# The second score product of an LSH attention read as bf16 halves of f32 words

## The chip, the cores and the metric

One core of a Trainium2 chip runs the whole program in one launch. The metric is the device time of one execution in microseconds; the median of three runs of the kernel before is 961.33 us (959.22 to 962.11).

## The reference

For four batches and eight heads, q, k and v are 768 x 64 in f32. Each row of q and k is hashed into six bits, the signs of its products with a 64 x 6 matrix; a query sees only keys with the same six bits.

```python
q_bits = (einsum(q, proj) > 0);  k_bits = (einsum(k, proj) > 0)      # six bits each
mask   = q_bucket[:, :, :, None] == k_bucket[:, :, None, :]
scores = where(mask, (q @ k.T) / sqrt(64), -1e9)
attn   = exp(scores - max(scores)); attn = attn / (sum(attn) + 1e-9)
x      = (attn @ v)                      # heads side by side: 3072 x 512
h      = maximum(x @ w_in, 0)            # 512 -> 2048
out    = (s * h * h + b) @ w_out         # 2048 -> 512
```

## The kernel before

The work is cut into 32 visits (batch and head) and each visit into three chunks of 256 queries: 96 slots of two tiles of 128 queries. Every result of a matmul goes through one PSUM tile, `bank`, with eight banks of 512 f32 columns.

*Scores* (`weights`, L600 to L650). For a tile of 128 queries the 768 keys are taken in two halves `g` of 384 columns, each in a bank of its own. A half is one accumulation of two matmuls with f32r operands, and this pair is one step of the plan. q and k are both split into a high part, rounded to f32r, and the rest, the low part. L615 multiplies 128 rows: the high part of q, twice (`aq`, the weights), with the high part of k and under it the low part of k (`ks[0]`). L616 multiplies 76 rows: the low part of q in rows 0 to 63 and twelve rows of masks (`bq[0:HR]`, the weights), with the high part of k and twelve mask rows (`ks[1][0:HR]`). The mask rows hold 0 and plus or minus 2^30, so a pair of different hashes gets a large negative score. `bq` and `ks` are f32r tiles that DVE, ACT and DMAs fill in `prep`; they lie in SBUF as four-byte words. There are 192 tiles, 384 halves, and so 384 matmuls each of L615 and L616, each with a weight load of its own.

VectorE then takes the maximum of both halves (L620), ScalarE the exponential and its sum (L621), GpSimd divides (L640). In the first ten visits the attention weights are transposed on TensorE (L672) and multiplied with v in f32 (L680); in the others they are split into two f16 parts (L647, L648), transposed by DMA (L649) and multiplied with v in f16 (L686, L692).

*The MoE layers* (`moe`). The first layer is three f16 matmuls per product, of 256 columns (L788 to L790); the second is f32r with 512 columns (L815). Both have 128 x 128 weights. This work is offered to the planner between the slots and fills TensorE behind the scores; after the last score at 786 us only it is left.

*The order.* All steps are first collected in a `Plan` with an engine, a cost in microseconds, the buffers that they read and write, and a priority. `order` (L73) then plays the program through with these costs and writes down the order in which each engine gets its steps; the engines' instruction streams follow this list. The cost of a score step is given at L617 by `mmc(HS, 2)`, that is 2 x (384 / 2286 + 0.0075) = 0.351 us. The sequence of L615 and L616 inside a step is fixed, and the two steps `g` of a tile have the same priority.

Of the kernel before, what the change touches and what calls it, by code (L numbers as in the profile page):

```python
# [14 lines left out]
BF16 = mybir.dt.bfloat16  # L15
# [153 lines left out]
def lsh_attention_moe(ctx: ExitStack, tc, q, k, v, proj, w_in, w_out, s, b, out):  # L169
    nc = tc.nc  # L170
# [5 lines left out]
    HS = S // 2  # L176
# [7 lines left out]
    HR = D + MR  # L184
# [10 lines left out]

    def f32(ap):
        return ap.bitcast(F32)

    def tile_(name, shape, dt=F32):
        return const.tile(shape, dt, name=name)  # L200

    def dma(dst, src, r, w, pr, size=0):

        plan.add(SP, 0.7, lambda: nc.sync.dma_start(f32(dst()), f32(src())), r, w, pr, size / RATE_DMA)

    def pe(cost, fn, r, w, pr):
        plan.add(PE, cost, fn, r, w, pr)

    def dve(n, fn, r, w, pr, ns=None):
        plan.add(DVE, ((n + 64) / 960.0 if ns is None else ns), fn, r, w, pr)  # L210

    def act(n, fn, r, w, pr, more=0.0, late_=0.0):
        plan.add(ACT, 0.21 + n / 1470.0 + more, fn, r, w, pr, late_)

    def pool(n, fn, r, w, pr, ns=None):
        plan.add(POOL, (0.08 + n / 430.0 if ns is None else ns), fn, r, w, pr)
# [14 lines left out]
    def mmc(n, c):  # L231
        return c * (n / 2286.0 + 0.0075)
# [26 lines left out]
    def late(w):  # L259
        return w >= FULL  # L260

    def TK(r, part, n):

        k = 6 // n
        return [("t", r, z) for z in range(part * k, (part + 1) * k)]

    def tring(i):

        return (i - PAIR) % 3 if i >= PAIR else i % 2
# [8 lines left out]
    def ering(j):  # L278

        return j % NE if late(slots[j // TPC][3]) else j % (NE + 2)  # L280
# [34 lines left out]
    pjk, pjq, pjm = [pjs[:, z] for z in range(3)]  # L315
    nc.vector.tensor_copy(pjh, pj[:, 0])
    nc.vector.tensor_tensor(pjl, pj[:, 0], f32(pjh), ALU.subtract)
    nc.vector.tensor_copy(pjk[0:D], pj[0:D, 1])
    nc.vector.tensor_copy(pjk[D:P], pj[D:P, 0])
    nc.vector.tensor_tensor(pjm[0:D], pj[0:D, 1], f32(pjk[0:D]), ALU.subtract)  # L320
    nc.vector.tensor_copy(pjq, pj[:, 1])
    nc.vector.tensor_tensor(pjq[D:P], pj[D:P, 1], f32(pjq[D:P]), ALU.subtract)
# [127 lines left out]
    def AK(x, r=(0, 1), g=(0, 1)):  # L450
        return [("aq", x, i, j) for i in r for j in g]

    def BK(x, r=(0, 1), g=(0, 1)):
        return [("bq", x, i, j) for i in r for j in g]

    def KK(x):
        return [("ks", x, i, g) for i in range(3) for g in range(2)]
# [142 lines left out]
    def weights(i, pr):  # L600

        bb, h, c, w = slots[i]
        x, y = w % 2, i % NST
        aq, bq, ks = AQ[x], BQ[x], KS[x]
        nm, z, rz, u, big_ = [st[:, y, m] for m in range(5)]
        nk, zk = [[("st", y, m, a) for a in range(TPC)] for m in range(2)]
        for a in range(TPC):
            t, j = c * TPC + a, TPC * i + a
            b0 = (6 if i < EARLY else TWO if late(w) else 0) if j % 2 else 0
            bk = [("b", b0), ("b", b0 + 1)]  # L610
            ts = slice(t * P, (t + 1) * P)
            for g in range(2):
                def mm(g=g, ts=ts, b0=b0):
                    cols, o = slice(g * HS, (g + 1) * HS), bank[:, b0 + g, 0:HS]
                    nc.tensor.matmul(o, aq[:, ts], ks[0][:, cols], start=True, stop=False)  # L615
                    nc.tensor.matmul(o, bq[0:HR, ts], ks[1][0:HR, cols], start=False, stop=True)  # L616
                pe(mmc(HS, 2), mm, AK(x) + KK(x) + BK(x), [bk[g]], pr)  # L617
            e, ek = EB[ering(j)], EK[ering(j)]
            sc = bank[:, b0:b0 + 2, 0:HS]
            dve(S, lambda a=a, sc=sc: nc.vector.tensor_reduce(nm[:, a:a + 1], sc, AX.XY, ALU.max, negate=True), bk, [nk[a]], pr, 0.88)  # L620
            act(S, lambda a=a, sc=sc, e=e: nc.scalar.activation(e.rearrange("p (g n) -> p g n", g=2), sc, AF.Exp, bias=nm[:, a:a + 1], accum_out=z[:, a:a + 1]),  # L621
                bk + [nk[a]], [ek, zk[a]], pr, 0.15, 0.2)

        def missing():
            nc.gpsimd.tensor_scalar(big_, nm, -FLOOR, 1e30, ALU.is_gt, ALU.mult)  # L625
            nc.gpsimd.tensor_scalar(u, nm, -FLOOR, 1.0 / (S + EPS), ALU.is_gt, ALU.mult)
        pool(TPC, missing, nk, [("st", y, 3), ("st", y, 4)], pr, 0.7)

        def inverse():
            nc.vector.scalar_tensor_tensor(rz, z, EPS, big_, ALU.add, ALU.add)  # L630
            nc.vector.reciprocal(rz, rz)  # L631
        dve(1, inverse, zk + [("st", y, 4)], [("st", y, 2)], pr, 0.32)
        for a in range(TPC):
            j = TPC * i + a
            e, ek = EB[ering(j)], EK[ering(j)]
            n, r = j % 2, tring(i)
            hi, lo, hk = pb[:, n, 0], pb[:, n, 1], EK[NE + n]

            def norm(eng, a=a, e=e):
                eng.tensor_scalar(e, e, rz[:, a:a + 1], u[:, a:a + 1], ALU.mult, ALU.add)  # L640
            ways = [(POOL, NORM, lambda norm=norm: norm(nc.gpsimd))]
            if not late(w) and not POOLN:
                ways.append((ACT, 0.93, lambda a=a, e=e: nc.scalar.activation(e, e, AF.Identity, bias=u[:, a:a + 1], scale=rz[:, a:a + 1])))
            plan.any(ways, [("st", y, 2), ("st", y, 3)], [ek], pr)
            if not late(w):
                continue
            act(S, lambda e=e, hi=hi: nc.scalar.mul(hi, e, TOP), [ek], [hk], pr)  # L647
            dve(S, lambda e=e, hi=hi, lo=lo: nc.vector.scalar_tensor_tensor(lo, e, TOP, hi, ALU.mult, ALU.subtract), [ek, hk], [("lo", n)], pr, 1.0)  # L648
            plan.add(SP, TCOST, lambda a=a, n=n, r=r: nc.sync.dma_start_transpose(tb[:, r, a].rearrange("p h t q -> p (h t) q"), pb[:, n].rearrange("p h n -> p (h n)")),  # L649
                     [hk, ("lo", n)], TK(r, a, 2), pr, TLAG)  # L650
# [206 lines left out]
    for i in range(NSL):  # L857
        pr = 10.0 * i
        bb, h, c, w = slots[i]
        last = c == NCH - 1  # L860
        if last and w + 2 < len(visits):
            parts = prep(w + 2, i, pr)
        if c == h == 0 and bb + 1 < B:
            value_scale(bb + 1, pr + VLATE)
        weights(i, pr + WP)
        while nd[0] < min(ND, decodes(i)):
            decode(nd[0], pr + 15)
            nd[0] += 1
        now, parts = (parts, []) if not last else (parts[:2], parts[2:])
        values(i, pr + 5, now)  # L870
        for bb, h, c, w in [slots[x] for x in closed]:
            last = c == NCH - 1
            if last and w + 2 < len(visits):
                prep_values(w + 2, pr + 12)
            if h == H - 1:
                todo.append(moe(bb, c, 0, PASS if bb == 0 else NF // 4))
                if bb == 0 and last:
                    todo.extend(moe(bb, c2, PASS, NF // 4) for c2 in range(NCH))
        closed.clear()
        while todo and next(todo[0], True):  # L880
            todo.pop(0)
# [66 lines left out]
```

## Time and profile before

| | |
|---|---|
| median of three runs | 961.33 us |
| profiled execution | 960.13 us |
| its span, first to last instruction | 958.3 us |
| TensorE matmul busy | 921.6 us, 96% |
| ScalarE, GpSimd, VectorE busy | 656.7, 614.2, 606.2 us |
| L615, 384 matmuls | 146.7 us busy, mean 382 ns |
| L616, 384 matmuls | 132.1 us busy, mean 344 ns |

The profiled execution is one run, with 1.8 us outside its span. Matmuls are pipelined: the next starts before the end that is drawn for the one before, so a mean duration is longer than the distance between two starts, and it is the distances that add up to time. A weight load (PEld) is an instruction of its own and can run while the matmul before is still streaming. "Issue" as a releaser means that an engine waited for nothing that the profile shows.

### The profile page before, as it was taken

The numbers are of one execution on the slowest core, as the hardware profiler recorded it, in microseconds if no ns is written. First come the engines' busy times: TensorE is split into PE (matmuls) and PEld (weight loads), VectorE is DVE, ScalarE is ACT, GpSimd is POOL, SyncE is SP. The second block draws the span as 40 slices with busy tenths as digits, with TensorE's granted clock in tenths as the row PEclk, the third lists the DMA queues.
The fourth block names the chain that finished last, engine by engine and source line by source line (L and its number), as shares of the span: only waits on it lengthen the run. The fifth ranks groups of instructions, "written<-read, shape, count | busy, mean of one in ns | idle before, by whom it ended". The sixth has DMA issues, their size and how long they took to land.

```text
span 958.3 us, 18093 instructions
## 1 busy us (share of the span) xinstructions
PE 921.6 (96%) x6512; PEld 733.2 (77%) x6512; DVE 606.2 (63%) x1001; ACT 656.7 (69%) x1234; POOL 614.2 (64%) x706
## 2 busy tenths in 40 slices
PE   7999887999999999999999999999999999999997
PEld 5876666677667777877878778788778887888886
DVE  7688997888777777776767676768777752000000
ACT  3788886778786777677778777767777775444342
POOL 2467775686896756766777676767667775334332
PEclk8999999899999999999999999999999999999999
DMA  5378657647779898997898798888887875100000
GB/s 123 87 232 220 177 160 191 179 133 209 174 153 204 176 206 181 204 213 149 157 204 172 163 204 163 177 174 167 186 173 149 171 134 105 55 19 27 12 23 23
DMA packets 303721, 144.44 MB, mean 151 GB/s; under 512 B 264256, under 2 KB 286784, under 8 KB 303632
## 3 DMA queue, kind: packets, MB, share of 16 engines
q1 hardware_dynamic: 298432, 126.25, 60.5%
q10 hardware_dynamic: 5200, 17.05, 5.7%
q8 instruction: 51, 0.84, 0.3%
q14 instruction: 38, 0.31, 0.1%
HBM read 51.38 MB, written 14.16 MB: 68 GB/s over the span
## 4 chain that ended last, share of the span: by engine, by line
PE 70%; DVE 9%; POOL 7%; ACT 5%; issue 5%; DMA 2%; POOLq 0%; SPq 0%; ACTq 0%; DVEq 0%
PE bank L815 22%; PE bank L788 7%; PE bank L790 7%; PE bank L789 7%; PE bank L615 6%; PE bank L616 5%; PE bank L686 4%; PE bank L680 3%; PE bank L672 2%; PE bank L692 2%; POOL eb L640 2%; DVE st L620 2%; PE bank L485 2%; POOL glb L802 2%; ACT eb L621 1%
## 5 line engine op out<-in xcount | busy, mean ns | idle before, releaser
L640 POOL TENSOR_SCALAR eb<-eb,st 128x768 f32<-128x768 f32 x176 | 200.4, 1145 | 68.4 <-DVE st L631 51.8
L815 PE MATMUL bank<-w,ghb 128*128 128x512 f32 x768 | 213.6, 406 | 0.0
L788 PE MATMUL bank<-xc,wi 128*128 128x256 f16 x768 | 211.6, 276 | 0.3 <-ACT rb L798 0.3
L620 DVE TENSOR_REDUCE st<-bank 128x1 f32<-128x768 f32 x192 | 180.3, 952 | 49.6 <-PE bank L616 42.3
L790 PE MATMUL bank<-xc,wi 128*128 128x256 f16 x768 | 209.7, 273 | 0.0
L789 PE MATMUL bank<-xc,wi 128*128 128x256 f16 x768 | 209.7, 273 | 0.0
L621 ACT ACTIVATE eb<-bank,st 128x768 f32<-128x768 f32 x176 | 157.5, 896 | 65.2 <-DVE st L620 29.3
L801 POOL TENSOR_SCALAR rb<-rb,misc 128x512 f32<-128x512 f32 x96 | 84.8, 884 | 154.0 <-ACT ghb L800 146.4
L648 DVE SCALAR_TENSOR_TENSOR pb<-eb,pb 128x768 f16<-128x768 f32 x132 | 144.3, 1097 | 61.5 <-ACT pb L647 60.9
L798 ACT ACTIVATE rb<-bank,dsc 128x512 f32<-128x512 f32 x95 | 65.2, 687 | 149.1 <-PE bank L790 135.4
L615 PE MATMUL bank<-ks,aq 128*128 128x384 f32 x384 | 146.7, 382 | 10.8 <-ACT eb L621 5.2
L815 PEld LDWEIGHTS bank<-w,ghb 128*128 128x128 f32 x768 | 136.1, 189 | 21.2 <-issue 0.4
L802 POOL TENSOR_TENSOR glb<-rb,ghb 128x512 fp32r<-128x512 f32 x96 | 137.1, 1428 | 5.8
L616 PE MATMUL bank<-ks,bq 76*128 76x384 f32 x384 | 132.1, 344 | 0.8 <-DMA bq<-nat 0.8
L647 ACT ACTIVATE pb<-eb 128x768 f16<-128x768 f32 x132 | 110.1, 836 | 14.3 <-DMA tb<-pb 13.3
L815 PE MATMUL bank<-w,glb 128*128 128x512 f32 x384 | 113.0, 402 | 3.1 <-POOL glb L802 3.1
L788 PEld LDWEIGHTS <-wi 128*128 128x128 f16 x768 | 75.0, 98 | 44.5 <-issue 37.3
L615 PEld LDWEIGHTS bank<-ks,aq 128*128 128x128 f32 x384 | 74.5, 194 | 30.0 <-ACT eb L621 9.2
L838 DVE COPY osb<-bank 128x256 f32<-128x256 f32 x4 | 1.5, 420 | 133.7 <-PE bank L815 133.0
L815 PEld LDWEIGHTS bank<-w,glb 128*128 128x128 f32 x384 | 70.8, 189 | 19.5 <-POOL glb L802 4.9
L625 POOL TENSOR_SCALAR st<-st 128x2 f32<-128x2 f32 x96 | 41.8, 436 | 63.2 <-DVE st L620 58.4
L790 PEld LDWEIGHTS <-wi 128*128 128x128 f16 x768 | 75.2, 98 | 8.6
(137 smaller groups left out, 1510.2 us busy)
## 6 DMA issues: line engine op xcount, KB each, us to landing
ks<-aq SPq DMA_DIRECT2D x60, 192.0 KB
raw<-in_moe_w_in_dram ACTq DMA_DIRECT2D x16, 512.0 KB
raw<-in_moe_w_out_dram ACTq DMA_DIRECT2D x16, 512.0 KB
xc<-xd SPq DMA_DIRECT2D x60, 128.0 KB
nat<-in_q_dram SPq DMA_DIRECT2D x32, 192.0 KB
nat<-in_k_dram SPq DMA_DIRECT2D x32, 192.0 KB
vm<-in_v_dram SPq DMA_DIRECT2D x32, 192.0 KB
xd<-xsb SPq DMA_DIRECT2D x48, 128.0 KB
```

The lines of the kernel that those rows point to most:

```text
L615: nc.tensor.matmul(o, aq[:, ts], ks[0][:, cols], start=True, stop=False)
L616: nc.tensor.matmul(o, bq[0:HR, ts], ks[1][0:HR, cols], start=False, stop=True)
L620: dve(S, lambda a=a, sc=sc: nc.vector.tensor_reduce(nm[:, a:a + 1], sc, AX.XY, ALU.max, negate=True), bk, [nk[a]], pr, 0.88)
L621: act(S, lambda a=a, sc=sc, e=e: nc.scalar.activation(e.rearrange("p (g n) -> p g n", g=2), sc, AF.Exp, bias=nm[:, a:a + 1], accum_out=z[: ...
L640: eng.tensor_scalar(e, e, rz[:, a:a + 1], u[:, a:a + 1], ALU.mult, ALU.add)
L647: act(S, lambda e=e, hi=hi: nc.scalar.mul(hi, e, TOP), [ek], [hk], pr)
L648: dve(S, lambda e=e, hi=hi, lo=lo: nc.vector.scalar_tensor_tensor(lo, e, TOP, hi, ALU.mult, ALU.subtract), [ek, hk], [("lo", n)], pr, 1.0)
L788: nc.tensor.matmul(hp, w[:, 0, fs], xc[:, 0, :], start=(cc == 0), stop=False)
L789: nc.tensor.matmul(hp, w[:, 1, fs], xc[:, 0, :], start=False, stop=False)
L790: nc.tensor.matmul(hp, w[:, 0, fs], xc[:, 1, :], start=False, stop=(cc == NC_ - 1))
L802: pool(2 * CH, lambda r=r, gh=gh, gl=gl: nc.gpsimd.tensor_tensor(gl, r, f32(gh), ALU.subtract), [rk, hk], [lk], MP)
L815: nc.tensor.matmul(o, (gh, gh, gl)[z][:, ts], w[:, z % 2], start=(f == fa and z == 0), stop=(f == fz - 1 and z == 2))
```

## The change

L616 reads its two operands as bf16. `top` takes a four-byte operand, views it as pairs of two-byte values, and selects the second of each pair, which is the upper half of the word: sign, exponent and the first seven bits of the fraction. The values are cut off, not rounded, and nothing is written: the same tiles are read with a step of four bytes. The mask values 0 and plus or minus 2^30 are the same in bf16. L615 stays f32r, and both accumulate into the same f32 bank. The cost of the step in the plan falls by 0.013.

```diff
+    def top(ap):
+
+        return ap.bitcast(BF16).rearrange("p (n t) -> p n t", t=2)[:, :, 1]
+
...
                     nc.tensor.matmul(o, aq[:, ts], ks[0][:, cols], start=True, stop=False)
-                    nc.tensor.matmul(o, bq[0:HR, ts], ks[1][0:HR, cols], start=False, stop=True)
-                pe(mmc(HS, 2), mm, AK(x) + KK(x) + BK(x), [bk[g]], pr)
+                    nc.tensor.matmul(o, top(bq[0:HR, ts]), top(ks[1][0:HR, cols]), start=False, stop=True)
+                pe(mmc(HS, 2) - 0.013, mm, AK(x) + KK(x) + BK(x), [bk[g]], pr)
```

## Rows read from the trace of the kernel before

**Rows 1.** Page, section 1: busy time, share of the span, instructions of each engine.

```profile
PE 921.6 (96%) x6512; PEld 733.2 (77%) x6512; DVE 606.2 (63%) x1001; ACT 656.7 (69%) x1234; POOL 614.2 (64%) x706
```

**Rows 2.** Page, section 2: the span in 40 slices, busy tenths of TensorE.

```profile
PE   7999887999999999999999999999999999999997
```

**Rows 3.** Three windows: length, busy us (instructions), clock, DMA share, GB/s.

```profile
0.00:250.00 250.00, 225.18 (x1749) 175.75 (x1750) 206.99 (x417) 190.11 (x414) 159.82 (x210) 0.96 0.63 171
250.00:786.00 536.00, 529.83 (x3656) 422.47 (x3655) 387.30 (x566) 392.72 (x711) 384.75 (x429) 1.00 0.84 177
786.00:958.30 172.30, 166.58 (x1111) 134.95 (x1110) 11.91 (x20) 73.85 (x112) 69.66 (x69) 1.00 0.17 40
```

**Rows 4.** Chain that ended last, share of the span by line (cut there).

```profile
by line: PE bank L815 21.6%; PE bank L788 7.0%; PE bank L790 6.7%; PE bank L789 6.7%; PE bank L615 6.1%; issue 5.3%; PE bank L616 5.3%; PE bank L686 4.0%; PE bank L680 2.6%; PE bank L672 2.4%; PE bank L692 2.3%; POOL eb L640 2.3%; DVE st L6
```

**Rows 5.** Groups by line: busy us, mean ns; idle before, what ended it.

```profile
L788 PEld LDWEIGHTS <-wi 128*128 128x128 f16 x768 | 75.0, 98 | 44.5 <-issue 37.3 <-DMA xc<-xd 0.3
L616 PEld LDWEIGHTS bank<-ks,bq 76*128 76x128 f32 x384 | 74.8, 195 | 2.8 <-issue 1.1
```

**Rows 6.** Timeline, PE, scores: start us, us, engine, line, operation, tiles, shape.

```profile
503.69 0.34 PE L616 MATMUL bank<-ks,bq 76*128 76x384 f32 x1
...
504.40 0.34 PE L616 MATMUL bank<-ks,bq 76*128 76x384 f32 x1
504.58 0.28 PE L788 MATMUL bank<-xc,wi 128*128 128x256 f16 x1
504.70 0.27 PE L789 MATMUL bank<-xc,wi 128*128 128x256 f16 x1
```

**Rows 7.** Timeline, PE, second layer of the MoE near 850 us, same columns.

```profile
849.22 0.27 PE L790 MATMUL bank<-xc,wi 128*128 128x256 f16 x1
849.25 2.11 PE L815 MATMUL bank<-w,ghb 128*128 128x512 f32 x8
851.20 1.09 PE L815 MATMUL bank<-w,glb 128*128 128x512 f32 x4
852.12 0.28 PE L788 MATMUL bank<-xc,wi 128*128 128x256 f16 x1
852.24 0.27 PE L789 MATMUL bank<-xc,wi 128*128 128x256 f16 x1
...
854.64 0.27 PE L790 MATMUL bank<-xc,wi 128*128 128x256 f16 x1
```

**Rows 8.** Timeline, PE weight loads, end of a group of scores near 512 us.

```profile
511.63 0.19 PEld L615 LDWEIGHTS bank<-ks,aq 128*128 128x128 f32 x1
...
512.16 0.10 PEld L788 LDWEIGHTS <-wi 128*128 128x128 f16 x1 [0.16 <-issue]
512.18 0.10 PEld L789 LDWEIGHTS <-wi 128*128 128x128 f16 x1
```

**Rows 9.** Timeline, PE matmuls of the same stretch.

```profile
511.34 0.27 PE L790 MATMUL bank<-xc,wi 128*128 128x256 f16 x1
...
511.63 0.35 PE L616 MATMUL bank<-ks,bq 76*128 76x384 f32 x1
...
511.99 0.34 PE L616 MATMUL bank<-ks,bq 76*128 76x384 f32 x1
512.17 0.28 PE L788 MATMUL bank<-xc,wi 128*128 128x256 f16 x1
512.29 0.27 PE L789 MATMUL bank<-xc,wi 128*128 128x256 f16 x1
```

**Rows 10.** Timeline, PE, first and last of the 73 places with f16 behind L616.

```profile
152.78 0.34 PE L616 MATMUL bank<-ks,bq 76*128 76x384 f32 x1
...
153.07 0.27 PE L789 MATMUL bank<-xc,wi 128*128 128x256 f16 x1
...
780.41 0.34 PE L616 MATMUL bank<-ks,bq 76*128 76x384 f32 x1
...
780.71 0.27 PE L789 MATMUL bank<-xc,wi 128*128 128x256 f16 x1
```

## The prediction

> **What bounds the kernel now.** I read the busy shares first. TensorE's matmuls are busy for 96% of the span, and no other engine passes 69% [rows 1]. The slices show where the missing 4% lies: in the first quarter and at the very end; from about 300 us to the end nearly every slice is full [rows 2]. [...] "Busy" is padded by pipelining, so I then read the chain of waits: its largest parts are lines of TensorE, and the two score lines, L615 and L616, are 6.1% and 5.3%, together 11.4% of 958.3 us, or 109 us [rows 4]. So a shorter score matmul is worth something in most places, though not in all. The changed line has 384 matmuls, each with a weight load of its own [rows 5]. Drawn durations overlap with their neighbours'; what counts is the distance from one start to the next, and that I read from the timeline.
>
> **The paces.** Five score matmuls in a row, from 503.69 to 504.58, are 0.178 us apart (384 columns, f32r) [rows 6]. Twenty-two f16 matmuls of 256 columns, from 852.24 to 854.64, are 0.1091 us apart. The twelve f32r matmuls of 512 columns before them start when the L790 of 849.22 is through (849.33) and end at 852.12: 2.79 us, 0.2325 each [rows 7]. From 384 to 512 columns f32r thus pays 0.0545 us for 128 columns, and f16 pays 0.1091 / 2 = 0.0546 for 128. The pace per column is the same. What f32r costs more is a fixed piece per instruction: 0.178 less 1.5 times 0.1091 (0.1636) is 0.0144 us.
>
> **The change part by part.**
>
> *The matmul of L616 in bf16.* No row shows a bf16 matmul, or one that reads every other 16-bit word. The lower end of its pace is that of f16 carried to 384 columns, 0.1636 us; the upper end is the present 0.178, as the words lie in memory as before. I take 0.1636: the surplus of f32r does not grow with the columns, so it is not the reading of four bytes per column that costs. Saving: 0.0144 x 384 = 5.5 us of TensorE time.
>
> *The weight load of L616 in bf16.* Its record will shrink from 195 to something near the 98 ns of the f16 loads [rows 5]. That alone is worth nothing, for today it is hidden: the f32r load of L615 at 511.63 starts together with the matmul ahead of it, the L616 of 511.63 [rows 8, 9]. But the f16 load behind an f32r matmul is not hidden. The load of L788 behind the last L616 starts only at 512.16, after 0.16 us without a load, 0.01 us before its own matmul (512.17), whereas the next load, at 512.18, runs beside that matmul [rows 8, 9]. F16 matmuls with 128 columns of weights follow L616 at 73 places, the first at 152.78 and the last at 780.41 [rows 10], and the load row of L788 has 37.3 us of such idle time put down to "issue" [rows 5]. In time: from the last L616 to the second f16 matmul it is 0.30 us at 504.40, 511.99 and 780.41 and 0.29 at 152.78 [rows 6, 9, 10]; the two paces make 0.287. The starts are rounded to 0.01; the mean of the four, 0.2975, puts the uncovered load at 0.0105, and I take 0.011. The other way round, f16 to f32r, costs nothing that shows: from L790 at 511.34 to L616 at 511.63 is 0.29, against 0.287 [rows 9].
>
> Now every L616 stands behind an L615, which stays f32r. After the change 384 two-byte loads will stand behind f32r matmuls, and I expect each to be uncovered as those of L788 are: 0.011 x 384 = 4.2 us that must be paid back. A pair costs 0.0144 - 0.011 = 0.0034 us less than before, 1.3 us in all. The bounds of this term are 0 (the load hidden, as the f32 load is) and 0.098 (the whole record of an f16 load uncovered, 37.6 us in all); I stay with 0.011, the row with the same neighbours.
>
> *What follows L616.* At 73 places f16 work follows, and there the uncovered load of today goes, because two-byte work will stand on both sides: 73 x 0.011 = 0.8 us saved. Where f32r work follows (L615 itself 192 times), the bf16 to f32r step costs nothing, by the row above; its bounds are 0 and the same 0.011.
>
> *The planner.* The cost of a score step falls by 0.013 us, 384 times, 5.0 us of planned TensorE time. The planner picks the order of all five engines from these times, so the order may change anywhere after the first score step. Nothing in the trace prices that; as bounds I take a tenth of the matmul-free 36.7 us (24.8 + 6.2 + 5.7) either way, 3.7 us, and nothing as the value, because it has no preferred sign.
>
> *Nothing else moves.* The operands are read in place: no copy, no DMA, no wait, no new tile; VectorE, ScalarE and GpSimd do what they did. VectorE's maximum waits for the end of L616, which comes 0.003 us sooner.
>
> **The sum.** 1.3 + 0.8 = 2.1 us of TensorE time. The scores take 384 x 2 x 0.178 = 136.7 us, of which 109 are on the chain: a factor of 0.80. That leaves 1.7 us. Against the profiled execution, 960.13 us (958.3 us of span and 1.8 around it), that is 958.4; it ran 1.2 us under the median, so on the median of the runs I say **959.6 us**. What is late next is TensorE again; no other engine is near.
>
> [...]
>
> **The rivals.**
>
> *The load is hidden after all.* If a bf16 load with a step is started ahead as the f32 load at 511.63 is, the full 5.5 us remain, and the 0.8 at the borders with f16: 6.3 x 0.80 = 5.0 us, **956.3**. For it: the cover is there, 0.178 us of L615. Against it: no two-byte load behind an f32r matmul of the scores uses it.
>
> *Slower: the uncovered load takes longer with its step.* The place is the start of each L616, behind L615. If the 0.011 doubles, a pair costs 0.0076 more than now, 2.9 us, less 0.8, times 0.80: +1.7. At three times, 0.033, it is (7.1 - 0.8) x 0.80 = +5.0, **966.3**. It decides from about 0.026 us on, where the loss passes 2.9 us. For it: every two-byte load of the trace reads packed words. Against it: the f32 loads read words at the same places and keep up under matmuls of 0.178 us. The same side is reached if the matmul keeps 0.178: (4.2 - 0.8) x 0.80 = +2.7, 964.0.
>
> *The order decides.* The 0.013 in the planner moves steps so that TensorE waits more or less in the first 250 us: 3.7 off the forecast, 955.9 or 963.3. For it: 24.8 free us there. Against it: 0.013 us is small beside the steps of 0.3 to 1.4 us in the plan.
>
> *The change does not take:* if the operands still went as four-byte words, only the order would differ, **961.3**. The types in the diff speak against that, and I give it next to nothing.
>
> **The chances.** The forecast 0.45, its own range 958 to 961.5; the hidden load 0.20; the longer load, or the unchanged pace, 0.16; the order 0.17, half each way; no effect 0.02. A run of this kernel can tell 0.3%, 2.9 us, from no change; so faster means under 958.4, slower over 964.2. Faster: 0.06 of the forecast, 0.19 of the hidden load, 0.08 of the order: 0.33. Slower: 0.14 of the longer load, 0.05 of the order, 0.01 of the forecast: 0.20. The rest, 0.47, is within. For the range I take in the hidden load with some luck of the order, 954.5, and the longer load at three times, 966.
>
> **What would show it.** In the rows of L616: a matmul of type bf16, with its weight load near 0.1 us. Right, if in the timeline L616's load starts about 0.17 us after L615's matmul and not with it, so that the load row of L616 shows some 384 x 0.15 = 58 us of idle put down to "issue"; if L615 to L616 to the next L615 is 0.354 us; and if the first f16 load behind L616 starts ahead. The first rival shows as a load that starts with L615 and a pair of 0.342; the second as a pair of 0.368 or more. The prediction is wrong if the pair lies at either of these, or if the matmul-free time of the first 250 us differs by more than 3 us.

## The result, and the profile after

The changed kernel takes 972.08 us (median of 6 runs, 969.44 to 973.62), the kernel before 961.72 us beside it: a ratio of 1.0106, 95% interval 1.0089 to 1.0122. The forecast was 959.6 us, no measurable change, with a range from 954.5 to 966. The change makes the kernel 1.1% slower, and it does so by a way that the prediction had priced at nothing.

Lines are shifted by four from here on: L615 and L616 are now L619 and L620, VectorE's maximum L624, ScalarE's exponential L625, the f16 matmuls L792 to L794, the f32r ones of the second layer L819. From the page of the changed kernel, the row of [rows 1] and, at the end, the granted clock in 40 slices:

```profile
span 971.0 us, 18104 instructions
...
PE 930.3 (96%) x6512; PEld 696.5 (72%) x6512; DVE 621.0 (64%) x1017; ACT 654.2 (67%) x1222; POOL 600.1 (62%) x706
...
PEclk7999997799999999999999999999999999999999
```

TensorE is busy for 96% of a span that is 12.7 us longer. In the slices the clock's digit is 7 in the first and in the seventh and eighth, at 146 to 194 us. The windows of [rows 3], for the changed kernel (length, busy us and instructions of PE, PEld, DVE, ACT, POOL, then the clock):

```profile
0.00:250.00 250.00, 219.42 (x1637) 153.68 (x1638) 201.32 (x390) 177.97 (x392) 152.23 (x201) 0.92 0.59 160
250.00:786.00 536.00, 530.75 (x3666) 397.02 (x3665) 398.97 (x596) 393.19 (x704) 367.27 (x428) 1.00 0.88 179
786.00:971.00 185.00, 180.16 (x1213) 145.78 (x1212) 20.73 (x32) 83.04 (x127) 80.63 (x79) 1.00 0.20 46
```

In the first 250 us TensorE is without a matmul for 30.6 us (24.8 before), the granted clock is 0.92 (0.96 before), and 1637 matmuls are done where 1749 were. From 250 to 786 us the two kernels do the same amount, 3666 and 3656. So the kernel falls behind in the first quarter and has 1213 matmuls left after 786 us in place of 1111. The groups that answer to [rows 5], with L620's matmul (busy us, mean ns; idle before):

```profile
L620 PE MATMUL bank<-ks,bq 76*128 76x384 bf16 x384 | 136.0, 354 | 0.0
...
L792 PEld LDWEIGHTS <-wi 128*128 128x128 f16 x768 | 75.3, 98 | 35.5 <-issue 28.0 <-DMA xc<-xd 0.3
...
L620 PEld LDWEIGHTS <-bq 76*128 76x128 bf16 x384 | 38.3, 100 | 54.7 <-issue 38.0
```

The matmul is of type bf16, its load takes 100 ns instead of 195, and there are now 38.0 us of "issue" before it, which were 1.1. The timeline of a group of scores in the changed kernel, matmuls and then their weight loads (start us, duration us):

```profile
540.02 0.34 PE L619 MATMUL bank<-ks,aq 128*128 128x384 f32 x1
540.20 0.35 PE L620 MATMUL bank<-ks,bq 76*128 76x384 bf16 x1
540.24 0.48 PE L619 MATMUL bank<-ks,aq 128*128 128x384 f32 x1
540.56 0.35 PE L620 MATMUL bank<-ks,bq 76*128 76x384 bf16 x1
540.60 0.48 PE L619 MATMUL bank<-ks,aq 128*128 128x384 f32 x1
540.92 0.34 PE L620 MATMUL bank<-ks,bq 76*128 76x384 bf16 x1
```

```profile
540.20 0.10 PEld L620 LDWEIGHTS <-bq 76*128 76x128 bf16 x1 [0.16 <-issue]
540.20 0.20 PEld L619 LDWEIGHTS bank<-ks,aq 128*128 128x128 f32 x1
540.56 0.10 PEld L620 LDWEIGHTS <-bq 76*128 76x128 bf16 x1 [0.15 <-issue]
```

The load of L620 at 540.20 starts with its own matmul, after 0.16 us without a load, and the f32r load behind it starts at once: what [rows 8] showed for L788 now happens before each L620 (all 384 loads start within 0.02 us of their own matmul; in the kernel before none did, and the median load started 0.175 us ahead). From one L620 to the next it is 0.36 us. A pair is one L619 with its L620. From 250 us on, where a pair follows a pair at once, the distance from one second product to the next has a median of 0.363 us (125 places); in the kernel before it is 0.356 (127 places).

### The profile page after: what moved, and what is told of

It reads as the page before. It is cut to its first block, busy times and chain, and to the rows that moved or that the text cites. A ratio compares the mean times of both kernels' runs of the same rounds, so it can differ in the third digit from the quotient of the medians.

```text
span 971.0 us, 18104 instructions
## 1 busy us (share of the span) xinstructions
PE 930.3 (96%) x6512; PEld 696.5 (72%) x6512; DVE 621.0 (64%) x1017; ACT 654.2 (67%) x1222; POOL 600.1 (62%) x706
## 4 chain that ended last, share of the span: by engine, by line
PE 74%; DVE 10%; issue 5%; POOL 5%; ACT 4%; DMA 1%; POOLq 0%; DVEq 0%; SPq 0%; ACTq 0%
PE bank L819 23%; PE bank L792 7%; PE bank L794 7%; PE bank L793 7%; PE bank L619 6%; PE bank L620 6%; PE bank L690 4%; PE bank L684 3%; PE bank L696 2%; DVE st L624 2%; PE bank L676 2%; PE bank L489 2%; POOL glb L806 1%; ACT eb L625 1%; POOL eb L644 1%
## 5 line engine op out<-in xcount | busy, mean ns | idle before, releaser
L644 POOL TENSOR_SCALAR eb<-eb,st 128x768 f32<-128x768 f32 x176 | 191.8, 1096 | 62.1 <-DVE st L635 55.7
L819 PE MATMUL bank<-w,ghb 128*128 128x512 f32 x768 | 221.0, 415 | 0.0
L624 DVE TENSOR_REDUCE st<-bank 128x1 f32<-128x768 f32 x192 | 180.8, 952 | 57.7 <-PE bank L620 50.2
L792 PE MATMUL bank<-xc,wi 128*128 128x256 f16 x768 | 211.2, 275 | 0.8 <-ACT rb L802 0.8
L794 PE MATMUL bank<-xc,wi 128*128 128x256 f16 x768 | 209.8, 273 | 0.0
L625 ACT ACTIVATE eb<-bank,st 128x768 f32<-128x768 f32 x176 | 157.5, 895 | 61.0 <-DVE st L624 35.1
L805 POOL TENSOR_SCALAR rb<-rb,misc 128x512 f32<-128x512 f32 x96 | 81.4, 848 | 149.9 <-ACT ghb L804 142.1
L619 PE MATMUL bank<-ks,aq 128*128 128x384 f32 x384 | 152.2, 449 | 12.4 <-ACT eb L625 6.1
L819 PEld LDWEIGHTS bank<-w,ghb 128*128 128x128 f32 x768 | 136.1, 190 | 21.8 <-issue 1.2
L620 PE MATMUL bank<-ks,bq 76*128 76x384 bf16 x384 | 136.0, 354 | 0.0
L819 PE MATMUL bank<-w,glb 128*128 128x512 f32 x384 | 114.2, 406 | 1.3 <-POOL glb L806 1.3
L792 PEld LDWEIGHTS <-wi 128*128 128x128 f16 x768 | 75.3, 98 | 35.5 <-issue 28.0
L619 PEld LDWEIGHTS bank<-ks,aq 128*128 128x128 f32 x384 | 77.0, 201 | 29.0 <-ACT eb L625 10.0
L629 POOL TENSOR_SCALAR st<-st 128x2 f32<-128x2 f32 x96 | 45.6, 475 | 81.4 <-DVE st L624 70.5
L819 PEld LDWEIGHTS bank<-w,glb 128*128 128x128 f32 x384 | 71.3, 189 | 15.9 <-POOL glb L806 1.8
```

The lines of the kernel that those rows point to most:

```text
L620: nc.tensor.matmul(o, top(bq[0:HR, ts]), top(ks[1][0:HR, cols]), start=False, stop=True)
L792: nc.tensor.matmul(hp, w[:, 0, fs], xc[:, 0, :], start=(cc == 0), stop=False)
L794: nc.tensor.matmul(hp, w[:, 0, fs], xc[:, 1, :], start=False, stop=(cc == NC_ - 1))
L819: nc.tensor.matmul(o, (gh, gh, gl)[z][:, ts], w[:, z % 2], start=(f == fa and z == 0), stop=(f == fz - 1 and z == 2))
```

## The experiments

**Which of the two parts loses.** The diff has two parts, a type and a planned cost. The first kernel keeps the bf16 matmul and takes the cost back, so that each engine has exactly the order of steps of the kernel before:

```diff
-                pe(mmc(HS, 2) - 0.013, mm, AK(x) + KK(x) + BK(x), [bk[g]], pr)
+                pe(mmc(HS, 2), mm, AK(x) + KK(x) + BK(x), [bk[g]], pr)
```

> L616 in bf16 as in the change, but the planned cost of a score step as before (0.351), so that every engine has its steps in the order of the kernel before. Order theory (the loss comes from the order that the cost of 0.338 gives): some 1 to 3 us over the kernel before, 962.5 to 964.5, since a pair of score matmuls is 0.363 us instead of 0.355 in the changed kernel's trace, 0.008 x 384 = 3.1 us, less what the borders with f16 give back. Pace theory (the bf16 matmul makes the loss): 970 or more.

Measured: 961.42 us against 959.67 for the kernel before, ratio 1.0011 (0.9992 to 1.0030). In the trace the sequence of instructions is that of the kernel before on every engine. The second keeps the cost and takes the bf16 back; in the trace its order is that of the changed kernel on every engine:

```diff
-  nc.tensor.matmul(o, top(bq[0:HR, ts]), top(ks[1][0:HR, cols]), start=False, stop=True)
+  nc.tensor.matmul(o, bq[0:HR, ts], ks[1][0:HR, cols], start=False, stop=True)
```

> L616 in f32r as before, but the planned cost of a score step 0.338, so that every engine has its steps in the order of the changed kernel. Order theory: most of the loss is here, 968 to 971. Pace theory: no change from before, 960 to 963.

Measured: 970.02 us, ratio 1.0101 (1.0071 to 1.0131). The order theory holds: the order alone costs 1.0%, of 1.06% in all; the bf16 matmul costs 0.1%, which is not clear of nothing.

**Where the order loses.** Windows of the kernel before, of bf16 in the old order, and of f32r in the new order, in this sequence:

```profile
0.00:100.00 100.00, 90.03 (x691) 71.43 (x692) 80.27 (x166) 72.27 (x165) 55.97 (x87) 0.95 0.61 164
...
150.00:200.00 50.00, 43.77 (x339) 33.43 (x336) 43.04 (x90) 39.10 (x82) 34.84 (x41) 0.93 0.59 153
```

```profile
150.00:200.00 50.00, 43.69 (x342) 31.26 (x341) 42.91 (x89) 38.03 (x80) 33.93 (x40) 0.92 0.61 156
```

```profile
0.00:100.00 100.00, 86.71 (x639) 67.61 (x640) 80.80 (x163) 68.36 (x156) 51.70 (x81) 0.91 0.61 163
...
150.00:200.00 50.00, 39.60 (x263) 28.94 (x261) 34.42 (x68) 30.37 (x65) 25.45 (x31) 0.80 0.55 143
```

In its first 100 us the new order has done 639 matmuls where 691 were done. With the old order the stretch from 150 to 200 us looks as before, bf16 or not: 339 and 342 matmuls at a clock of 0.93 and 0.92. With the new order it has 263 at 0.80, and VectorE, ScalarE and GpSimd are idler too (VectorE 34.4 us busy instead of 43.0): no engine is busier than before, they wait for each other. Two such waits, in TensorE's timeline of the f32r kernel with the new order (in brackets the idle time and what ended it):

```profile
159.56 0.34 PE L620 MATMUL bank<-ks,bq 76*128 76x384 f32 x1
162.18 0.44 PE L619 MATMUL bank<-ks,aq 128*128 128x384 f32 x1 [2.29 <-ACT eb L625]
...
163.84 0.47 PE L676 MATMUL bank<-ident,eb 128*128 128x128 f32 x1 [0.68 <-POOL eb L644]
...
166.76 0.53 PE L620 MATMUL bank<-ks,bq 76*128 76x384 f32 x1
167.08 0.53 PE L619 MATMUL bank<-ks,aq 128*128 128x384 f32 x1
167.40 0.53 PE L620 MATMUL bank<-ks,bq 76*128 76x384 f32 x1
```

```profile
181.18 0.49 PE L489 MATMUL bank<-ident,nat 128*128 128x128 f32 x3
184.71 0.90 PE L489 MATMUL bank<-ident,nat 128*128 128x128 f32 x3 [3.03 <-DVE bq L492]
```

After the L620 of 159.56 the next step in TensorE's list is another score step, whose bank is not free until ScalarE's exponential of an earlier tile is done, and TensorE waits 2.29 us. After the L489 of 181.18 the list has another transposition that waits 3.03 us for VectorE's L492. The same time on VectorE:

```profile
181.53 0.93 DVE L436 SCALAR_TENSOR_TENSOR wi<-raw,wsc,wi 128x512 f16<-128x512 f32 x1
182.49 0.96 DVE L624 TENSOR_REDUCE st<-bank 128x1 f32<-128x768 f32 x1
183.37 0.76 DVE L752 SCALAR_TENSOR_TENSOR xsb<-xpb,vsc,xsb 128x256 f16<-128x256 f32 x1
184.05 0.60 DVE L492 SCALAR_TENSOR_TENSOR bq<-bank,misc,aq 128x384 fp32r<-128x384 f32 x1
```

VectorE's list puts the split of a MoE weight (L436), a maximum (L624) and an output split (L752) ahead of the L492 for which TensorE waits. And the loss has a second part. By the clock's records the granted clock falls to its lower level, 0.50 of full, at 163.3 us, 1.1 us after the end of the long wait and within the next one, and stays there until 177.0 us: from 166.76 to 167.40 the score matmuls are 0.32 us apart, not 0.178. Before 200 us TensorE is at that level for 20.5 us in the kernel before and for 37.5 us here; 6.9 us of the difference lie in the first 28 us. The first row of the page of this kernel, beside [rows 1], divides the loss:

```profile
PE 925.9 (96%) x6512; PEld 735.5 (76%) x6512; DVE 622.6 (64%) x1017; ACT 654.5 (68%) x1222; POOL 603.1 (62%) x706
```

The span is 10.1 us longer (968.4 us). TensorE is without a matmul for 42.4 us in place of 36.7, 5.7 us more, and the same 6512 matmuls are drawn 4.4 us longer. An estimate of the clock's part from the trace alone: matmuls are busy at the lower level for 32.2 us in place of 18.9; if all of them are drawn out there as the score matmuls are, from 0.178 us to 0.32, then 0.44 of the 13.3 us is the clock's, 5.9 us. So waits and clock have about equal parts in these two executions.

**Which stretch of the plan.** Both kernels are f32r; the cut of 0.013 is given to the first 21 slots alone, or to the others alone:

```diff
-  pe(mmc(HS, 2) - 0.013, mm, ...)
+  pe(mmc(HS, 2) - (0.013 if i < EARLY else 0.0), mm, ...)     # the second: 0.0 and 0.013 exchanged
```

> All f32r as before; the planned cost of a score step is 0.338 in the first 21 slots alone (to about 140 us), 0.351 after. Head theory (the loss of the changed order is made in the first 200 us, where TensorE waits and its clock falls): some 5 to 10 us over before, 965 to 970. Spread theory (the loss is summed up over all slots): 960 to 963.

> All f32r as before; the planned cost of a score step is 0.351 in the first 21 slots as before, 0.338 from slot 21 on. Head theory: the order up to some 140 us is that of before, so 959 to 963, unless the stretch from 150 to 200 us is hit by itself. Spread theory: 967 to 970.

Measured: 971.84 us (ratio 1.0116, 1.0089 to 1.0143) with the cut in the first slots, 963.18 us (1.0032, 1.0011 to 1.0052) with the cut in the rest. The head theory holds: a cut in slots up to 140 us is enough for the whole loss. The cut in the rest costs 0.3% by itself.

**Is it the size of the cut?** f32r in all three, with the cost lower by 0.006 and by 0.001, or higher by 0.013:

```diff
-  pe(mmc(HS, 2) - 0.013, mm, ...)
+  pe(mmc(HS, 2) - 0.006, mm, ...)                             # the others: + 0.013, - 0.001
```

> All f32r as before; the planned cost of a score step is cut by 0.006 everywhere instead of 0.013. If the plan answers to the cost smoothly: about half of the loss of order alone, 964 to 966. If any other cost means another order, with a loss that has no relation to the size of the cut: anywhere from 958 to 972, and the half-clock stretches before 200 us go with it.

> All f32r as before; the planned cost of a score step is 0.013 higher, 0.364, about what a pair in the changed kernel takes. If the plan answers smoothly and the cut was wrong because it is too short: faster than before or equal, 950 to 961. If any other cost means another order by chance: 958 to 972.

> All f32r; the planned cost of a score step is cut by 0.001 instead of 0.013. If the plan answers smoothly: 960 to 961.5, no change. If any other cost means another order, and the order of before is one of the better ones: 963 to 973, no nearer to before than the cuts of 0.006 and 0.013.

Measured: 973.72 us (1.0130, 1.0105 to 1.0154), 969.54 us (1.0097, 1.0067 to 1.0128), and, for the cut of 0.001, 976.93 us (1.0164, 1.0145 to 1.0182), the slowest of all. The cuts of 0.006 and 0.001 come out slower than the slowest that was expected of them, 972 and 973. The plan does not answer smoothly, nor to the sign. Each of these costs gave another order, and all six, whole or in part, are slower than that of the kernel before, by 0.3 to 1.6%. The kernel with the cut of 0.001, from 150 to 200 us:

```profile
150.00:200.00 50.00, 41.97 (x299) 31.48 (x299) 33.19 (x70) 31.29 (x68) 26.50 (x34) 0.86 0.54 146
```

299 matmuls at 0.86: the same kind of stretch as with the full cut.

**What the bf16 matmul costs by itself.** Two kernels in the order of before replace one operand of L616 by a packed bf16 tile of zeros, `pk`, and so leave out the second product (two added lines make L620 L622 here):

```diff
-  nc.tensor.matmul(o, top(bq[0:HR, ts]), top(ks[1][0:HR, cols]), start=False, stop=True)
+  nc.tensor.matmul(o, pk[0:HR, 0:P], top(ks[1][0:HR, cols]), start=False, stop=True)      # e3
+  nc.tensor.matmul(o, top(bq[0:HR, ts]), pk[0:HR], start=False, stop=True)                # e4
```

> Order of before, L616 in bf16; its weights are a packed tile of zeros (128 neighbouring two-byte values) instead of every other half of bq, so the low part of q and the masks are left out of the result. If the step of four bytes makes the weight load longer: the pair falls from 0.363 to about 0.354 us, the sum of 0.178, 0.1636 and an uncovered load of 0.011 to 0.013. If the step costs nothing in the load: it stays at 0.363.

> Order of before, L616 in bf16 with its weights read in steps of four bytes as in the change; the moving operand is a packed tile of zeros, so the product of the low part of q and the masks is left out of the result. If the step slows the moving operand: the pair falls from 0.363 to about 0.354 us. If the step costs only in the weight load: it stays at 0.363.

In one execution of each, the medians of 127 distances from one second product to the next, from 250 us on, are 0.365 us with both operands in steps of four bytes (the first experiment), 0.362 with packed weights, 0.357 with a packed moving operand. So it is mostly the moving operand for which the step costs, 0.008 us a matmul; the load has 0.003 of it. The packed tile holds zeros; no run has a packed operand with the real values, so that zeros by themselves are quicker is not ruled out. Two neighbouring second products, first of the kernel with both stepped, then with the moving operand packed:

```profile
529.45 0.35 PE L620 MATMUL bank<-ks,bq 76*128 76x384 bf16 x1
...
529.81 0.34 PE L620 MATMUL bank<-ks,bq 76*128 76x384 bf16 x1
```

```profile
528.40 0.34 PE L622 MATMUL bank<-pk,bq 76*128 76x384 bf16 x1
...
528.75 0.34 PE L622 MATMUL bank<-pk,bq 76*128 76x384 bf16 x1
```

If packed bf16 has the pace of f16, an estimate that no run tests, the 0.357 are 0.178 for f32r, 0.1636 for packed bf16, and 0.015 left for the uncovered load. The same sum with packed weights, 0.362 = 0.178 + 0.172 + 0.012, puts a packed load at 0.012.

**The border itself.** In the order of before, L615 reads the upper halves too; the lower bits of the high parts are then left out of the scores, which become coarser:

```diff
-  nc.tensor.matmul(o, aq[:, ts], ks[0][:, cols], start=True, stop=False)
+  nc.tensor.matmul(o, top(aq[:, ts]), top(ks[0][:, cols]), start=True, stop=False)
```

> Order of before; L615 too reads the upper halves of its four-byte words, so the lower bits of the high parts are left out of the result. If the weight load of L616 is uncovered because f32r stands ahead of it, and the moving operand in steps of four bytes costs 0.008 as the two looks with packed operands say: loads start with the matmul before them again, and a pair takes 2 x 0.172 = 0.344 us. If a two-byte load read in steps of four bytes is always uncovered: 2 x (0.172 + 0.015) = 0.374 us.

Matmuls, then weight loads, of this kernel:

```profile
521.14 0.34 PE L620 MATMUL bank<-ks,bq 76*128 76x384 bf16 x1
...
521.49 0.34 PE L620 MATMUL bank<-ks,bq 76*128 76x384 bf16 x1
...
521.83 0.34 PE L620 MATMUL bank<-ks,bq 76*128 76x384 bf16 x1
...
522.18 0.33 PE L620 MATMUL bank<-ks,bq 76*128 76x384 bf16 x1
```

```profile
521.14 0.10 PEld L619 LDWEIGHTS <-aq 128*128 128x128 bf16 x1
521.32 0.10 PEld L620 LDWEIGHTS <-bq 76*128 76x128 bf16 x1
```

Three pairs in 1.04 us, 0.346 by the median: 0.173 a matmul. The loads start with the matmul before their own, about 0.17 us ahead, as at 521.14. So a two-byte load in steps of four bytes is hidden in this run, where two-byte work stands ahead of it; in the changed kernel, behind f32r, none of the 384 is. The one execution took 951.45 us; more executions, beside the kernel before:

> The kernel of the look with both products in bf16 again, timed: order of before, and the bits of the high parts below the upper half of their words are left out of the scores. Border theory (f32r and two-byte work side by side cost the uncovered load, and bf16 by itself is the cheaper form): a pair of 0.342 to 0.344 us against 0.356 saves 384 x 0.012 = 4.6 us, and more at the borders with f16, so 953 to 957. If the 951.45 of the one look holds, there is a gain beside the pair as well.

Measured: 954.90 us against 960.41, ratio 0.9938 (0.9917 to 0.9959): the gain that the border theory forecast, though the pair is 0.346 us and not 0.342 to 0.344; and the only kernel of the study that beats the one before, at the price of coarser scores.

The last one keeps L615 in f32r and, in the order of before, puts the two L615 of a tile ahead of its two L616 where both halves stand side by side on TensorE:

```diff
-  for each half g, in its own step:  L615(g); L616(g)          # in outline
+  where the two steps are neighbours: L615(0); L615(1); L616(0); L616(1)
```

> Order of before, L616 in bf16; in the 124 tiles whose two halves stand next to each other on TensorE, both L615 come first and then both L616, so that one load in place of two stands uncovered. If an uncovered load costs 0.015 us: 124 x 0.015 x 0.8 = 1.5 us under the ungrouped kernel with the order of before, about 960 and no different from the kernel before. If the border costs nothing by itself: the same as that kernel, 961.4.

Measured: 960.37 us against 961.25, ratio 0.9993 (0.9980 to 1.0006). In its trace 260 loads of the second product start with their own matmul, and the 124 that stand behind another second product start 0.174 us ahead: hidden again, which is the mechanism without a change of type. The time is 0.18% below the ungrouped kernel's 1.0011, as the uncovered load would have it, but the two intervals overlap; it is no different from the kernel before.

## Why the prediction was wrong

*The planner* is the step that failed. The prediction said that "the order may change anywhere after the first score step", bounded that by 3.7 us either way, and took nothing as the value "because it has no preferred sign". Order alone costs 1.0%, some 10 us. Both halves of the argument failed. The bound, a tenth of the matmul-free time (24.8, 6.2 and 5.7 us by the windows of [rows 3]), had no row behind it: matmul-free time alone grew by 5.7 us with the new order, and the bound left out the clock: where 0.50 of it was granted, the score matmuls were 0.32 us apart and not 0.178. And for this kernel the sign was hardly open: six of six other orders lost. The prediction's own sign of being wrong came: the matmul-free time of the first 250 us is 30.6 us against 24.8, 5.8 apart where 3 were allowed. Against the rival "the order decides" it was held that 0.013 us "is small beside the steps of 0.3 to 1.4 us in the plan"; a cut of 0.001 moved the kernel by 1.6%. The rival had its place right, the first 250 us, and its price of 963.3 too low by 8.8 us.

*The weight load* went as foretold: it is uncovered behind L615, as [rows 8] showed for L788. The trace after has 54.7 us of idle time before L620's loads, 38.0 of it put down to "issue", where 58 were expected. Its price was 0.011; by the estimate with the pace of f16 it is 0.012 packed and 0.015 as read here.

*The matmul in bf16* was sized too fast. 0.1636 was the lower bound; 0.173 is measured where both products are bf16 (half of the 0.346), and 0.172 is what the estimate leaves beside f32r, both between the bounds. The argument that the surplus of f32r is a fixed piece, "so it is not the reading of four bytes per column that costs", does not carry over to bf16 in steps of four bytes: by the packed runs the step of the moving operand costs 0.008 us, over half of the 0.0144. With 0.172 and 0.015 a pair is 0.365 where 0.354 was forecast and 0.356 is the pair before: 0.009 x 384 = 3.5 us lost, where 1.3 us of gain were forecast.

*What follows L616* came as said: in the first experiment the second f16 matmul behind L620 comes 0.296 us after it in the median of 65 places: 0.015 for L620's own load, 0.172, and 0.109 for an f16 matmul whose load is hidden. In the changed kernel the "issue" time before L792's loads fell from 37.3 to 28.0 us, and the first f16 load behind L620 starts 0.173 us ahead of its own matmul (median of 76 places; 0.004 us in 72 places before).

*The sum without the planner* was thus off in two terms and had the wrong sign, by little: with the measured pair it is (3.5 - 0.8) x 0.80 = 2.2 us lost, where 1.7 were forecast as gained. Measured with the order held is 1.0011, with an interval that takes in no change; the forecast of 0.9982 lies just outside it. Forecast and measurement are near because every term is small, not because the two were sized rightly.

For the step of four bytes the runs show at most 0.003 us in the load (0.365 to 0.362), with a record of 100 ns, and 0.008 us in the 384 columns of the moving operand (0.365 to 0.357), by one execution each.

Still open: no run took the waits without the lower clock, so their equal parts in the 10 us are read from two traces and not separated by an experiment. Nor do the runs show why the order of the kernel before has less of both; that the planner's other constants suit this one cost better than any near it is possible and not tested.

## What to carry to other kernels

Where a planner writes the order of all engines from estimated costs, a cost is not a small correction: here a change of one by 0.001 us made another kernel, 1.6% slower. Measure a change of an instruction with the order held as it was, and a new order by itself, before adding the two up. And a narrower type in every second matmul was no saving here, where the neighbour kept the wide type (1.0011 with the order held; a pair of 0.365 us against 0.356), and only the kernel that changed both gained (0.9938; 0.346).

## What the runs showed of the hardware

A bf16 matmul with both operands in steps of four bytes takes 0.173 us for 384 columns where both products are bf16 (half of a pair's 0.346), against 0.178 for f32r (half of 0.356). Beside f32r it is 0.172 by estimate: the pair's 0.365 less 0.178 and less 0.015 for the load. That pair is 0.008 us shorter when the moving operand is packed (0.357, a tile of zeros). A two-byte weight load behind an f32r matmul starts with its own matmul here (all 384 loads of L620 in the changed kernel, within 0.02 us) and costs time that is not hidden: 0.010 us for f16 behind L616 in the kernel before (0.297 us in the median of 72 places less the 0.287 of the two paces), and for bf16 in steps of four bytes 0.015 us by estimate, the 0.357 less 0.178 and less the 0.1636 carried over from f16. Behind another two-byte matmul the load starts 0.17 us ahead, and the 0.346 us of such a pair is 0.002 over two of the 0.172.
